# Where the low parts of the first expert's first weights are made, in a two-layer mixture-of-experts kernel

## Chip, cores and metric

The program runs on one core of a Trainium2 chip. The metric is the device time of one execution in microseconds (us); lower is better.

## What is computed

An attention with 32 memory slots gives x, 4608 tokens of width 512. Two mixture-of-experts layers follow. In the first, every one of 8 experts gets exactly 576 tokens, by a greedy assignment in the order of the logits; in the second, every token goes to its best expert, with a gate. Cut to the first layer:

```python
logits = x @ w_gate
order = np.argsort(-logits.flatten())
for idx in order:
    tok, e = idx // E, idx % E
    if assigned[tok] >= 0 or counts[e] >= cap:
        continue
    assigned[tok] = e
    counts[e] += 1
for e in range(E):
    h = np.maximum(x[assigned == e] @ w1[e], 0.0)
    out[assigned == e] = h @ w2[e]
```

## The kernel before

Products of the expert layers need more than one float32r product: a weight piece of 512 KB (128 x 1024) is loaded as `wraw`, ScalarE writes its rounded part (`w0h` or `w1h`, "0" for w1 of the reference and "1" for w2), and another engine writes the rest, `w0l` or `w1l` = raw minus rounded part. `Weights.split` (line 1282) does both. Four pieces make one expert's matrix.

The program has three stretches. (1) Attention, to about 120 us. (2) The routing of the first layer, about 120 to 168 us: four rounds of `Route1.guess` on VectorE. In a round, `propose` makes each token's proposal (lines 400 to 404, operations over 128 x 288), `counts` (line 410) sums it over the tiles, TensorE sums over the lanes (line 390, tile `rt`), and seven small operations (lines 427 to 435) make the new cutoffs. Beside the rounds, `beside` (line 1694) has TensorE compute what rows of x are still missing (line 259, tile `tr`), ScalarE copy them out (line 261, `xr`), SP store them to `xd`, SP load the first expert's four `w0` pieces, and, through `split`, ScalarE make `w0h` and GpSimd make `w0l`. TensorE, ScalarE and SP have their order as written there (`QUEUES`); in a round the rows stand ahead of the sums over the lanes in TensorE's queue, 3 rows ahead of the first sum and 1 or none ahead of the second.

Then `expert0` (lines 693 to 709) and `tables` make the tokens of the first two slots of 288: `slot0` gives the indices of slot 0, on which GpSimd's three gathers of `rows` hang (line 1326), `slot1` those of slot 1 (line 766), and, inside it, `check` counts the proposers once more (line 410 on VectorE, line 390 on TensorE, lines 499 and 500) and sets a flag. All engines read the flag and branch on it (`rest`, lines 524 and 525); with the given data it is 0 and the further rounds are left out. `first_x` then turns the gathered rows into slot 0's x: three copies on VectorE (line 1336), transposes on TensorE (line 1340), rounded part on ScalarE (line 1342), rest on VectorE (line 1343); x lies where the `w1` parts will lie later and so is called w1h and w1l there. After it, ScalarE's queue loads the four `w1` pieces into the same four places of `wraw`.

(3) The slots, from 168 us to the end: `mm1` (lines 1371 to 1374) has eight steps f of 12 products, steps 2k and 2k+1 with piece k of w0; ScalarE (line 1376, `hh`) and VectorE (line 1377, `hl`) empty its four PSUM banks; `mm2` follows (lines 1385 to 1387). In slot 0 VectorE also makes tables for the other slots (lines 656 to 661, 777, 789), which TensorE multiplies (line 783) between the steps, in nine products to a group.

Of the kernel before, what the change touches and what calls it, by code (L numbers as in the profile page):

```python
# [14 lines left out]
B, H, S, D, M = 8, 8, 576, 64, 32       # batches, heads, tokens of a batch, head width, memory slots  # L15
P = 128
N = B * S                               # tokens
NT = N // P
DM = H * D
E, F = 8, 1024                          # experts, their width  # L20
# [6 lines left out]
# pieces of the rows of x that a step computes, at three places  # L27
# [3 lines left out]
def chunks(b):  # L31
    """Token tiles of a batch: (tile, first lane, last lane, first s)."""
    if b % 2 == 0:
        t = b * S // P
        return [(t + i, 0, P, i * P) for i in range(4)] + [(t + 4, 0, 64, 512)]
    t = (b * S - 64) // P
    return [(t, 64, P, 0)] + [(t + 1 + i, 0, P, 64 + i * P) for i in range(4)]


def attention(tc, kv, qT, phiT, wg_sb, ident, xd, lg, keep, work, psum):  # L40
    """Logits of all tokens into lg. Returns what computes the rows of x of a batch, from
    the attention weights and value sums that stay in `keep`."""
# [31 lines left out]
    def ahead(s):  # L74
        """What step s is to use, in that order."""
        for f, b in ((load_q, s), (load_kv, s + 1), (load_phi, s + 2)):
            if 0 <= b < B:
                f(b)
# [21 lines left out]
    def a2(b):  # L100
# [3 lines left out]
        for j0 in range(0, 5, 2):  # L104
            js = list(range(j0, min(5, j0 + 2)))
            pt = psum.tile([P, 512], FT, name="tr", bufs=3).rearrange("p (a g c) -> p a g c", a=2, g=2)
            for j in js:
                t, l0, l1, s0 = cs[j]
                n = l1 - l0
                for g in range(2):  # L110
                    if n == P:
                        nc.tensor.transpose(pt[:, j - j0, g], e[:, g, s0:s0 + P], ident)
                    else:
                        # the lanes keep their place: out rows l0..l1
# [40 lines left out]
    def a4b(b):  # L155
# [3 lines left out]
        # keys: head u of a pair on partitions 64u.., columns 32u..  # L159
# [33 lines left out]
    def half(i, k, mid, end):  # L193
        """VectorE's part of a half's softmax: the first part of i beside the second part of k."""
# [5 lines left out]
        if k is not None:  # L200
# [5 lines left out]
            # column = token's place in the tiles of 128  # L206
# [139 lines left out]
def bc_e(a):  # L346
    """[128, 8] over the token tiles."""
    return a[:, None, :].to_broadcast([P, NT, E])


def bc_t(a):
    """[128, 36] over the experts."""
    return a[:, :, None].to_broadcast([P, NT, E])


class Route1:
    """Every expert takes its 576 best of the tokens that its betters left.

    A token proposes to the best expert whose cutoff it reaches. An expert never takes a
    token below the 576th of those that propose to it, so its cutoff can be raised to any  # L360
    value that 576 of its proposers reach; once no expert has more than 576 proposers, they
    are the greedy assignment."""

    def __init__(self, tc, pool, psum, lg, cn):
# [11 lines left out]
        # -1 on the lane itself and those before  # L376
# [9 lines left out]
    def total(self, src, n):  # L386
        """Sums over the lanes, on every lane."""
# [24 lines left out]
    def guess(self, first, beside):  # L412
        """A new cutoff, the proposers' mean, where there are too many of them."""
# [23 lines left out]
    def step(self):  # L437
        """The same, but only where 576 or more reach the pivot; between the cutoff and `hi`
        the pivots halve what is left."""
# [26 lines left out]
        # a new cutoff where 576 or more of too many proposers reach the pivot  # L466
# [10 lines left out]
        # below the pivot, or from the top again where 576 have come to lie above  # L477
# [11 lines left out]
    def check(self):  # L489
        """flag = 1 unless every expert has 576 proposers, which then are the assignment:  # L490
        each token is with one expert, and all that it would rather be with are full of
        better ones, however the cutoffs came about."""
# [4 lines left out]
        ps = self.total(part[:, 0:8], 8)  # L497
        d = self.tmp("d", [1, 24])
# [3 lines left out]
    def resolve(self, beside, per=4):  # L502
        """Some rounds; what they come to is the assignment if the flag, which check() sets, is 0."""
# [4 lines left out]
    def rest(self, after, blocks=8, per=4):  # L508
        """Where the flag is set: rounds until it isn't, at last one expert after the other; then after()."""
# [21 lines left out]
    def general(self):  # L531
        """One expert is filled at a time, at the highest logit at which one gets full;
        of equal logits there the first tokens are taken."""
# [18 lines left out]
        def first_of(x, w):  # L552
            # of the entries that are 1, the first expert's
            v.tensor_tensor(x, x, w, op=OP.mult)

        with tc.For_i(0, E + 1):
# [43 lines left out]
            # everything above the level, and as many at it as the expert still takes  # L600
# [19 lines left out]
    def ranks(self, src):  # L620
        """How many entries of the same expert come before, in the order of the tokens."""
# [3 lines left out]
def lane_sums(r1, src):  # L625
    """Of src [128, tile, expert]: sums over the lanes, and less those of the lane itself and the later ones."""
# [8 lines left out]
def prefix(r1, sums, per_expert):  # L635
    """Of a src of 0 and 1: the count of ones in earlier tiles or lower lanes,
    per expert, or with the experts before it (per_expert False); [128, tile, expert]."""
# [13 lines left out]
def split_pos(nc, tmp, pos, cn, oh):  # L651
    """pos div 32, and in oh the one-hot of pos mod 32."""
# [12 lines left out]
def pause(n):  # L665
    """Steps without work, for an engine to get done what the next one reads."""
    for _ in range(n):
        yield


class Invert1:
    """From the assignment to the tokens of the positions: idx [(q, t'), block of 32 positions]
    = 4 token + q, and in tok the token's lane and tile for the partition (s mod 4, t'),
    column (s div 4, block in slot)."""
# [11 lines left out]
    def expert0(self, beside=lambda: None):  # L686
        """The first expert's tokens alone, which are those of the first two slots."""
# [9 lines left out]
        # the place, from 1024 on; 0 where the token is another expert's  # L697
# [13 lines left out]
    def places(self):  # L711
        """The place of every token."""
# [8 lines left out]
    def slot(self, s):  # L721
        """[mod 32, (lane, 128 tile), block] of the tokens of a slot's positions."""
# [18 lines left out]
    def slot0(self, beside=lambda: None):  # L741
        """The first slot's tokens: position 128 c + lane at (lane, c)."""
# [14 lines left out]
    def slot1(self, beside=lambda: None):  # L757
        """The second slot's part of idx."""
# [9 lines left out]
    def all(self, r2):  # L768
# [33 lines left out]
        # the lane and the tile of the token, for each quarter of the partitions  # L802
# [12 lines left out]
def constants(tc, pool, ident=None):  # L815
# [27 lines left out]
    # rep[k, a, 32 q + t] = 1 where k = 32 a + t  # L843
    rep = t("rep", [64, 2, P], FT)
    rt = t("rept", [64, P], FT)
    for a in range(2):
        # (column mod 32) + 32 a - k
# [7 lines left out]
NS = 23                     # slots of 288 that 8 experts can need for 4608 tokens  # L855
NE = 27                     # columns of tokens, of 36, that are through six experts
AS = 5                      # slots that they fill for certain
G = 9
# [7 lines left out]
class Route2:  # L866
    """Every token to its best expert; the experts' tokens fill slots of 288.

    Tokens lie in the first layer's order: lane (s mod 4, t), column (s div 4, block).
    A token's place is its rank with its expert, moved by whole slots."""  # L870
# [30 lines left out]
    def choose(self, j0, j1):  # L901
        """The first of the best experts for the columns j0..j1."""
# [19 lines left out]
    def gates(self, j0, j1):  # L922
        """Softmax of the choice times sigmoid of its output gate, in three bfloat16 parts."""
# [29 lines left out]
    def ranks(self, j0, j1, before):  # L953
        """Of the tokens of the columns j0..j1: rank with their expert, as (div 32, mod 32)."""
# [47 lines left out]
    def left(self, j0):  # L1002
        """One-hot (place mod 32) times what the place is to know, for G columns."""
# [18 lines left out]
    def per_token(self, c, a, out):  # L1022
        """a [128, 8] of the tokens' experts."""
# [8 lines left out]
    def slots(self, k, tab, w):  # L1032
        """The slots before each expert's, from how many it has; the slots' experts.

        k may go twice over the experts."""
# [731 lines left out]
```

## Time and profile before

| what | us |
|---|---|
| median of the runs | 1065.51 |
| all three runs | 1065.51, 1063.35, 1068.17 |
| span of the profiled execution, first to last instruction | 1063.4 |
| attention and what comes before the routing | 0 to about 120 |
| routing of the first layer, to slot 0's first product | about 120 to 168 |
| slots of both layers | 168 to 1063.4 |

The profiled execution is listed with its span alone; the span is within 0.1 us of the lowest of the three runs and 2.1 us below their median, so that hardly any time lies around it. Over the span TensorE is busy 990.5 us (93%), VectorE 663.7 (62%), ScalarE 486.4 (46%) and GpSimd 565.6 (53%). In the table of windows and in timelines, PE is TensorE's products, PEld its weight loads, DVE VectorE, ACT ScalarE, POOL GpSimd; an arrow with an engine names what ended the idle time before an instruction. PEclk is the granted clock of TensorE, 1.00 for 2.4 GHz and 0.50 for 1.2 GHz.

### The profile page before, as it was taken

To read this page: it belongs to the slowest core of one execution; us is meant where nothing else is said; L and a number is where in the kernel's file an instruction comes from. 1 tells how busy PE (TensorE), PEld (TensorE's weight loads), DVE (VectorE), ACT (ScalarE), POOL (GpSimd) and SP (SyncE) were. 2 spreads that over 40 slices of the span, in tenths; PEclk is the share of its full clock that TensorE was granted. 3 is DMA by queue.
4 is the path that set the end of the run, shared out by engine and by line. 5 is a ranking of instruction groups with operands and counts; after the bars stand their busy time and mean duration, and the time that the engine had idled before them with its cause. 6 is when DMAs were issued, how large, how long until landed. Compare 5 with 4: busy or idle time off the path is not lost. (4 is left out here: it accounts for less than half of the span.)

```text
span 1063.4 us, 21285 instructions
## 1 busy us (share of the span) xinstructions
PE 990.5 (93%) x8163; PEld 936.4 (88%) x8163; DVE 663.7 (62%) x1181; ACT 486.4 (46%) x906; POOL 565.6 (53%) x545
## 2 busy tenths in 40 slices
PE   6778968999999999999999999999999898989974
PEld 4555648999999999999999999999999898989962
DVE  3888875554545454547964798666665665656641
ACT  3546623343434333333333557555555554546530
POOL 3102033243434343434443487778887787878875
PEclk9889967999999999999999999999999999989987
DMA  8999744344343435352525656566666565656663
GB/s 311 367 339 298 237 142 139 120 129 141 108 140 109 147 102 151 102 162 85 152 95 160 189 193 207 185 203 216 201 204 219 183 201 181 204 180 201 201 211 115
DMA packets 77544, 192.16 MB, mean 181 GB/s; under 512 B 13884, under 2 KB 32320, under 8 KB 76400
## 3 DMA queue, kind: packets, MB, share of 16 engines
q1 hardware_dynamic: 62448, 158.93, 46.1%
q0 software_dynamic: 14400, 29.59, 8.5%
q10 hardware_dynamic: 576, 2.10, 0.5%
q8 instruction: 69, 1.13, 0.4%
q14 instruction: 51, 0.42, 0.1%
HBM read 162.25 MB, written 28.44 MB: 179 GB/s over the span
## 5 line engine op out<-in xcount | busy, mean ns | idle before, releaser
L1385 PE MATMUL py<-hh,w1h 128*128 128x288 f32 x1024 | 304.7, 298 | 12.4 <-DVE yr L1397 12.4
L1386 PE MATMUL py<-hl,w1h 128*128 128x288 f32 x1024 | 305.6, 298 | 0.1
L1387 PE MATMUL py<-hh,w1l 128*128 128x288 f32 x1024 | 305.0, 298 | 0.0
L1371 PE MATMUL ph<-xh,w0h 128*128 128x288 f32 x992 | 273.0, 296 | 0.0
L1372 PE MATMUL ph<-xh,w0l 128*128 128x288 f32 x992 | 271.5, 296 | 0.0
L1318 POOL DMA_INDIRECT xg<-xd,idx x135 | 147.8, 1095 | 217.9 <-DVE xt L1349 151.1
L1376 ACT ACTIVATE hh<-ph 128x288 fp32r<-128x288 f32 x256 | 104.9, 411 | 232.3 <-PE ph L1374 232.1
L1385 PEld LDWEIGHTS py<-hh,w1h 128*128 128x128 f32 x1024 | 195.7, 191 | 13.9 <-DVE yr L1397 13.6
L1386 PEld LDWEIGHTS py<-hl,w1h 128*128 128x128 f32 x1024 | 195.5, 191 | 0.5 <-DVE hl L1377 0.5
L1377 DVE SCALAR_TENSOR_TENSOR hl<-ph,hh 128x288 fp32r<-128x288 f32 x256 | 116.1, 454 | 127.5 <-ACT hh L1376 127.3
L1387 PEld LDWEIGHTS py<-hh,w1l 128*128 128x128 f32 x1024 | 195.6, 191 | 0.0
L1371 PEld LDWEIGHTS ph<-xh,w0h 128*128 128x128 f32 x992 | 186.4, 188 | 2.4 <-issue 2.1
L1372 PEld LDWEIGHTS ph<-xh,w0l 128*128 128x128 f32 x992 | 186.4, 188 | 0.2 <-issue 0.2
L1374 PE MATMUL ph<-xl,w0h 128*128 128x288 f32 x992 | 171.3, 294 | 0.0
L1318 POOL DMA_INDIRECT xg<-x2d,r2gidxB x118 | 145.8, 1235 | 36.4 <-issue 32.3
L1286 DVE TENSOR_TENSOR w0l<-wraw,w0h 128x1024 fp32r<-128x1024 f32 x96 | 117.0, 1218 | 48.8 <-ACT w0h L1285 48.7
L1374 PEld LDWEIGHTS ph<-xl,w0h 128*128 128x128 f32 x992 | 145.2, 188 | 0.0
L1286 DVE TENSOR_TENSOR w1l<-wraw,w1h 128x1024 fp32r<-128x1024 f32 x100 | 120.6, 1206 | 24.8 <-ACT w1h L1285 24.7
L1485 POOL DMA_INDIRECT out_dram<-yr,r2sidxB x99 | 117.8, 1189 | 32.0 <-issue 18.9
L1285 ACT ACTIVATE w1h<-wraw 128x1024 fp32r<-128x1024 f32 x100 | 105.4, 1054 | 46.3 <-PE py L1386 25.1
L1285 ACT ACTIVATE w0h<-wraw 128x1024 fp32r<-128x1024 f32 x100 | 103.4, 1050 | 0.4 <-DMA wraw<-in_u_dram 0.4
L1394 ACT ACTIVATE yT<-py 128x288 f32<-128x288 f32 x64 | 26.4, 412 | 128.5 <-PE py L1387 128.5
(319 smaller groups left out, 1056.6 us busy)
## 6 DMA issues: line engine op xcount, KB each, us to landing
wraw<-in_u_dram SPq DMA_DIRECT2D x140, 512.0 KB, 4.2
wraw<-in_w_dram SPq DMA_DIRECT2D x60, 512.0 KB, 3.7
kvt<-in_kv_dram SPq DMA_DIRECT2D x16, 1024.0 KB, 15.8
q<-in_qT_dram SPq DMA_DIRECT2D x8, 1152.0 KB, 18.4
x2d<-yr SPq DMA_DIRECT2D x64, 144.0 KB, 2.4
xd<-xr SPq DMA_DIRECT2D x32, 256.0 KB, 2.6
ph<-in_phiT_dram SPq DMA_DIRECT2D x8, 576.0 KB, 18.3
xg<-xd,idx POOLq DMA_INDIRECT x135
```

Source lines behind the costliest of these rows:

```text
L1285: self.nc.scalar.activation(h, r, AF.Copy)
L1286: (eng or self.nc.vector).tensor_tensor(l, r, h.bitcast(FT), op=OP.subtract)
L1318: self.nc.gpsimd.indirect_dma_start(out=x[:, j], out_offset=None, in_=src, in_offset=bass.IndirectOffsetOnAxis(ap=idx[:, j:j + 1], axis=0))
L1371: nc.tensor.matmul(ps, wh[:, o + c], xh[:, c], start=(c == 0), stop=False)
L1372: nc.tensor.matmul(ps, wl[:, o + c], xh[:, c], start=False, stop=False)
L1374: nc.tensor.matmul(ps, wh[:, o + c], xl[:, c], start=False, stop=(c == 3))
L1376: nc.scalar.activation(hh[:, f], ps, AF.Relu)
L1377: nc.vector.scalar_tensor_tensor(hl[:, f], ps, 0.0, hh[:, f].bitcast(FT), op0=OP.max, op1=OP.subtract)
L1385: nc.tensor.matmul(ps, wh[:, f], hh[:, f], start=(f == 0), stop=False)
L1386: nc.tensor.matmul(ps, wh[:, f], hl[:, f], start=False, stop=False)
L1387: nc.tensor.matmul(ps, wl[:, f], hh[:, f], start=False, stop=(f == 7))
L1485: i = nc.gpsimd.indirect_dma_start(out=os, out_offset=bass.IndirectOffsetOnAxis(ap=idx[:, j:j + 1], axis=0), in_=y[:, j], in_offset=None, ...
```

## The change

`split` takes which parts it is to make, and the low part is always VectorE's. In the rounds only the rounded parts are made. Piece 0's low part is put into `check`, between the product that sums the count over the lanes and the operation that reads this sum. The low parts of pieces 1 to 3 come behind `first_x`, ahead of the loads of the `w1` pieces.

```diff
-    def split(self, which, k, eng=None):
+    def split(self, which, k, parts="hl"):
         r = self.raw()[:, k].rearrange("p a b -> p (a b)")
         h, l = (a[:, k].rearrange("p a b -> p (a b)") for a in self.all(which))
-        self.nc.scalar.activation(h, r, AF.Copy)
-        (eng or self.nc.vector).tensor_tensor(l, r, h.bitcast(FT), op=OP.subtract)
+        if "h" in parts:
+            self.nc.scalar.activation(h, r, AF.Copy)
+        if "l" in parts:
+            self.nc.vector.tensor_tensor(l, r, h.bitcast(FT), op=OP.subtract)
...
-    def check(self):
+    def check(self, beside=lambda: None):
...
         ps = self.total(part[:, 0:8], 8)
+        beside()
         d = self.tmp("d", [1, 24])
...
                     if 0 < k < 5 and i == 0:
-                        w.split(0, k - 1, nc.gpsimd)
+                        w.split(0, k - 1, "h")
...
-                def tables():
+                def tables(beside=lambda: None):
                     inv.slot0(inv.places)
-                    inv.slot1(r1.check)
+                    inv.slot1(lambda: r1.check(beside))
...
+                def low(ks):
+                    for k in ks:
+                        w.split(0, k, "l")
...
                 with tc.manual_schedule(engines=ALL):
-                    tables()
+                    tables(lambda: low((0,)))
                 r1.rest(again)
                 with tc.manual_schedule(engines=ALL):
                     sl.first_x(rows0, cols0, psum, cn["ident"])
+                    low((1, 2, 3))
                     for k in range(4):
                         w.load(1, k, 0, queue=nc.scalar)
```

Line numbers of the changed kernel are up to 3 higher here: 1289 is its line of the low part, 1281 that of a load, 1339, 1346 and 1380 answer to 1336, 1343 and 1377, and 500, 501 and 767 to 499, 500 and 766.

GpSimd's queue from the routing's first constants to the read of the flag, before:

```order
L381 IOTA r1m_1579 128x648
L1286 TENSOR_TENSOR w0l_1657<-wraw_1589,w0h_1656 128x1024 x4
L1326 DMA rows_1834<-xd,idx_1781 128x512 x2
L1326 DMA rows_1834<-xd,idx_1781 32x512
L524 TENSOR_LOAD r1flag
```

and after:

```order
L380 IOTA r1m_1578 128x1152
L381 IOTA r1m_1579 128x648
L1329 DMA rows_1830<-xd,idx_1778 128x512 x2
L1329 DMA rows_1830<-xd,idx_1778 32x512
L525 TENSOR_LOAD r1flag
```

The four subtractions are gone from GpSimd; its next work is the gathers.

VectorE around the check (`r1td` reads the summed count), before:

```order
L730 TENSOR_TENSOR r1tR_1898<-r1tR_1898,c_tile_83 128x324
L410 TENSOR_REDUCE r1tpart<-r1prop 128x8
L499 TENSOR_SCALAR r1td<-rt 1x8
L500 TENSOR_REDUCE r1flag<-r1td 1x1
L766 TENSOR_SCALAR idx_1782<-rt,c_q 128x9
L524 TENSOR_LOAD r1flag
```

and after:

```order
L731 TENSOR_TENSOR r1tR_1894<-r1tR_1894,c_tile_83 128x324
L410 TENSOR_REDUCE r1tpart<-r1prop 128x8
L1289 TENSOR_TENSOR w0l_1657<-wraw_1589,w0h_1656 128x1024
L500 TENSOR_SCALAR r1td<-rt 1x8
L501 TENSOR_REDUCE r1flag<-r1td 1x1
L767 TENSOR_SCALAR idx_1779<-rt,c_q 128x9
L525 TENSOR_LOAD r1flag
```

One subtraction stands between the count over the tiles and the read of its sum over the lanes.

VectorE from slot 0's x into slot 0's products, before:

```order
L1336 COPY cols_1835<-rows_1834 32x512
L1343 TENSOR_TENSOR w1l_4090<-tr,w1h_4089 128x4x128 x2
L1343 TENSOR_TENSOR w1l_4090<-tr,w1h_4089 128x4x32
L1377 SCALAR_TENSOR_TENSOR hl_4172<-ph_4173,hh_4171 128x288
L656 TENSOR_SCALAR r2xhi<-pos 128x36
```

and after:

```order
L1339 COPY cols_1831<-rows_1830 32x512
L1346 TENSOR_TENSOR w1l_4087<-tr,w1h_4086 128x4x128 x2
L1346 TENSOR_TENSOR w1l_4087<-tr,w1h_4086 128x4x32
L1289 TENSOR_TENSOR w0l_1657<-wraw_1589,w0h_1656 128x1024 x3
L1380 SCALAR_TENSOR_TENSOR hl_4172<-ph_4173,hh_4171 128x288
L657 TENSOR_SCALAR r2xhi<-pos 128x36
```

Three subtractions stand ahead of the first `hl`.

ScalarE's queue at the same place, with the engines whose semaphores each instruction waits for, before:

```order
L1342 ACTIVATE w1h_4089<-tr 128x4x128 [waits PE_49] x2
L1342 ACTIVATE w1h_4089<-tr 128x4x32 [waits PE_49]
L1280 DMA wraw_1589<-in_w_dram 128x1024 [waits Pool_49] x4
L1376 ACTIVATE hh_4171<-ph_4173 128x288 [waits DVE_49,PE_49]
L1376 ACTIVATE hh_4171<-ph_4174 128x288 [waits PE_49]
```

and after:

```order
L1345 ACTIVATE w1h_4086<-tr 128x4x128 [waits PE_49] x2
L1345 ACTIVATE w1h_4086<-tr 128x4x32 [waits PE_49]
L1281 DMA wraw_1589<-in_w_dram 128x1024 [waits DVE_49] x3
L1281 DMA wraw_1589<-in_w_dram 128x1024 [waits DVE_49,Activation_49]
L1379 ACTIVATE hh_4171<-ph_4173 128x288 [waits PE_49]
```

The four loads of `w1`, which overwrite what the subtractions read, waited for GpSimd and now wait for VectorE, each for its piece, and the first `hh` is queued behind them.

## Rows read from the trace of the kernel before

**Rows 1.** The first line of the page.

```profile
span 1063.4 us, 21285 instructions
```

**Rows 2.** Windows: per engine busy us (instructions), then PEclk, DMA share, GB/s.

```profile
138.00:140.00 2.00, 2.00 (x6) 1.43 (x5) 1.86 (x5) 0.60 (x1) 0.00 (x0) 0.50 0.00 0
169.00:1064.00 895.00, 861.73 (x6740) 847.80 (x6739) 537.46 (x895) 407.79 (x724) 527.79 (x459) 0.98 0.51 164
```

**Rows 3.** Timeline of GpSimd in the routing: start, us, engine, line, what, idle before.

```profile
129.81 2.34 POOL L1286 TENSOR_TENSOR w0l<-wraw,w0h 128x1024 fp32r<-128x1024 f32 x1 [23.86 <-ACT w0h L1285]
133.19 2.46 POOL L1286 TENSOR_TENSOR w0l<-wraw,w0h 128x1024 fp32r<-128x1024 f32 x1 [1.04 <-ACT w0h L1285]
143.90 2.36 POOL L1286 TENSOR_TENSOR w0l<-wraw,w0h 128x1024 fp32r<-128x1024 f32 x1 [8.24 <-ACT w0h L1285]
147.83 2.63 POOL L1286 TENSOR_TENSOR w0l<-wraw,w0h 128x1024 fp32r<-128x1024 f32 x1 [1.57 <-ACT w0h L1285]
```

**Rows 4.** Timeline of VectorE in the routing.

```profile
125.25 0.46 DVE L401 SCALAR_TENSOR_TENSOR r1masked<-r1tlt,lg 128x288 f32<-128x288 f32 x1
129.95 2.52 DVE L401 SCALAR_TENSOR_TENSOR r1masked<-r1tlt,lg 128x288 f32<-128x288 f32 x1
134.07 1.90 DVE L422 TENSOR_TENSOR r1tpv<-r1masked,r1prop 128x288 f32<-128x288 f32 x1
142.35 0.17 DVE L427 TENSOR_SCALAR r1tu<-rt 128x8 f32<-128x8 f32 x1 [1.67 <-PE rt L390]
143.91 2.37 DVE L435 TENSOR_TENSOR r1cut<-r1cut,r1tu 128x8 f32<-128x8 f32 x1
148.89 0.19 DVE L700 TENSOR_TENSOR r1tx<-r1tx,lg 128x36 f32<-128x36 f32 x1
149.11 1.42 DVE L701 TENSOR_TENSOR r1tx0i<-r1tx,r1prop 128x36 int32<-128x36 f32 x1
```

**Rows 5.** Timeline of TensorE in the routing.

```profile
128.65 2.84 PE L259 MATMUL tr<-vbd,eT 128*128 128x256 f32 x12
136.75 5.45 PE L259 MATMUL tr<-vbd,eT 128*128 128x256 f32 x12
152.70 2.27 PE L733 MATMUL rt<-r1tR,r1toh 128*32 128x18 bf16 x36 [1.38 <-DVE r1tR L730]
```

**Rows 6.** Timeline of VectorE from the check into slot 0.

```profile
159.24 0.15 DVE L499 TENSOR_SCALAR r1td<-rt 1x8 f32<-1x8 f32 x1 [1.90 <-PE rt L390]
164.71 1.10 DVE L1336 COPY cols<-rows 128x512 f32<-128x512 f32 x3 [4.08 <-DVEq L525]
167.83 0.89 DVE L1343 TENSOR_TENSOR w1l<-tr,w1h 128x512 fp32r<-128x512 f32 x2 [0.16 <-ACT w1h L1342]
171.82 0.46 DVE L1377 SCALAR_TENSOR_TENSOR hl<-ph,hh 128x288 fp32r<-128x288 f32 x1 [3.10 <-ACT hh L1376]
180.83 0.59 DVE L789 TENSOR_SCALAR r2R<-c_i,r2sm 128x144 bf16<-128x144 bf16 x3
211.19 1.23 DVE L1286 TENSOR_TENSOR w0l<-wraw,w0h 128x1024 fp32r<-128x1024 f32 x1 [0.55 <-ACT w0h L1285]
```

**Rows 7.** Timeline of GpSimd: last gathers of `rows` and of slot 1, one beside VectorE's subtraction.

```profile
159.59 0.88 POOL L1326 DMA_INDIRECT rows<-xd,idx  x1 [0.30 <-issue]
175.18 1.37 POOL L1318 DMA_INDIRECT xg<-xd,idx  x1 [0.30 <-issue]
211.60 1.63 POOL L1318 DMA_INDIRECT xg<-xd,idx  x1 [0.30 <-issue]
```

**Rows 8.** Timelines in slot 0: ScalarE's loads and first `hh`; TensorE.

```profile
167.77 1.90 ACTq L1280 DMA_DIRECT2D wraw<-in_w_dram  x4
171.37 0.41 ACT L1376 ACTIVATE hh<-ph 128x288 fp32r<-128x288 f32 x1 [3.33 <-PE ph L1374]
...
173.37 0.29 PE L1371 MATMUL ph<-w1h,w0h 128*128 128x288 f32 x1
181.35 0.75 PE L783 MATMUL rt<-r2R,r2L 128*64 128x144 bf16 x9
```

## Prediction

> **What bounds the kernel now.** I read the windows by stage first, then the timelines of the engines in the routing. In the slots TensorE is busy 861.73 of 895 us [rows 2]: there it is the bound, and whatever lets the first slot begin earlier moves the end by as much, since all later work hangs on its products in a fixed order. So the question is what sets slot 0's start. In the routing that is one chain on VectorE: each round needs the cutoffs of the one before, the indices need the last proposals, the gathers need the indices, the branch needs the flag.
>
> In that chain the reader is to see four operations that last far longer than their like. Line 401 takes 0.46 us in one round and 2.52 in the next, line 422, over the same 128 x 288, 1.90, line 435 2.37 where an operation of its size takes 0.17, and line 701 1.42 where its neighbour takes 0.19 [rows 4]. Laid beside GpSimd's timeline, each overlaps one of the four subtractions and ends within 0.4 us of it: 129.95 to 132.47 beside 129.81 to 132.15, 134.07 to 135.97 beside 133.19 to 135.65, 143.91 to 146.28 beside 143.90 to 146.26, 149.11 to 150.53 beside 147.83 to 150.46 [rows 3, 4]. I read this as VectorE being held until GpSimd's operation is over.
>
> The Trainium skill, page "SBUF — State Buffer", section "Who interferes with whom", says that a VectorE instruction with two SBUF inputs and a GpSimd instruction that reads SBUF exclude each other, the later one waiting for the whole of the earlier. The trace agrees: the four held ones read two SBUF tiles, and line 700, with one input in PSUM, is not held at 0.19 us [rows 4].
>
> **What is removed.** Four GpSimd subtractions of 2.34 to 2.63 us [rows 3]. GpSimd's own time is worth nothing, it idles there. VectorE's chain loses the stretch: 2.52 - 0.46 = 2.06, 1.90 - 0.46 = 1.44, 2.37 - 0.17 = 2.20, 1.42 - 0.19 = 1.23, together 6.93 us.
>
> A wait goes with it. In the fourth round VectorE idles 1.67 us for the sum over the lanes (line 427, [rows 4]), because TensorE has three rows of x in front of that sum, and they take 5.45 us where the same 12 products took 2.84 before [rows 5]: the granted clock was 0.50 at 138 to 140 us [rows 2], after TensorE had stood almost idle from 131.5 (128.65 + 2.84) to 136.75, waiting for VectorE. With the first two stretches gone (3.50 us), the sum behind which these rows stand, and with it the rows, come at 136.75 - 3.50 = 133.25 [rows 5]; the idle time shrinks from 5.2 to 1.7 us, and I take it that the clock stays up. Then the rows end at 133.25 + 2.84 = 136.1, and VectorE, which wants the sum at 142.35 - 1.67 - 3.50 = 137.2, doesn't wait: 1.67 us more. What is late next is the third row behind that sum: TensorE's next three rows (2.84 us) then end just about when the last proposals are ready, and I take off 0.3 for it, an estimate from these starts. Gain of the rounds and the first indices: 6.93 + 1.67 - 0.3 = 8.3 us.
>
> **What is added at the check.** One subtraction, 1.23 us on VectorE [rows 6]. It begins when the idle time ahead of line 499 begins, 159.24 - 1.90 = 157.34, and would end at 158.6; the sum is there at 159.24. So it costs nothing, with 0.7 us to spare. If that cover were gone, the flag would be late by at most 1.23. It does meet GpSimd's gathers: one beside a subtraction takes 1.63 against 0.88 [rows 7], so the last gather of rows ends at 161.2 instead of 160.5 (159.59 + 0.88). VectorE touches those rows only after the branch, at 164.71 [rows 6], and is held there by the branch: nothing again. The loads and stores on SP and ScalarE's rounded parts keep their order; GpSimd's queue only gets shorter.
>
> The Trainium skill's page "SBUF — State Buffer", section "A bandwidth-pool intuition that's wrong (but worth ruling out)", speaks against such a place: it gives about 620 ns for a GpSimd-issued DMA alone and 3100 ns beside a VectorE copy. By that figure one gather would be late by about 2.5 us, an estimate, and the sum worse by some 0.5; the row with 1.63 us [rows 7] bears out a much smaller delay for this very pair.
>
> **What is added behind x.** Three subtractions of 1.23, from the end of line 1343 at 167.83 + 0.89 = 168.72 to about 172.4 [rows 6]. Four waits follow. (a) Products of step 2 begin at 173.37 [rows 8] and want piece 1's low part, ready by 169.9; pieces 2 and 3 are wanted two and four steps later: no cost. (b) The loads of w1 now wait for VectorE, and the fourth leaves at 172.4 instead of within 167.77 to 169.67 [rows 8]; its piece is wanted by products over 20 us later: no cost. (c) Behind these loads on ScalarE stands the first `hh`, at 172.9 (172.4 and a quarter of 1.90) instead of 171.37 [rows 8], and with it VectorE's first `hl` and all that follows there is 1.5 us late. The PSUM bank that they empty is wanted again four steps on, after 176: no cost. (d) The tables that VectorE makes between those steps are late by about as much; the last three of TensorE's first group of nine end at 180.83 + 0.59 = 181.42, and the nine products run from 181.35 to 182.1 [rows 6, 8]. The ninth starts at about 182.0, so it has 0.6 us to spare and would be 0.9 late. I take 0.7, with a little caught up on the way, between 0 (VectorE catches up in time) and 1.5 (the whole lateness).
>
> **Sum.** 8.3 - 0.7 = 7.6 us. The profiled span of 1063.4 [rows 1] becomes 1055.8; from the median of the runs, 2.1 higher, 1065.5 - 7.6 = 1057.9.
>
> **Rivals.** *The clock stays up for longer.* With TensorE fed more densely up to the indices, the two groups of 36 small products that lead to the indices (2.27 us each, [rows 5]) could run at the upper level. Bounds: nothing, if their length isn't the clock's, to half of each, 2.3 us in all; with VectorE's chain in slot 0 capping what is won behind it, and 0.7 not lost, 10.6 us at most: 1054.9. Against it: TensorE waits for VectorE there in any case. 10%.
>
> *The clock falls all the same.* The rows show it at the lower level after 5.2 us almost idle; whether 1.7 us do it they don't show. Then the three rows take 5.45 again, the sum comes at 133.25 + 5.45 = 138.7, and of the 5.2 us by then won only 3.5 stay; the row behind the sum costs about 0.8 more (half of its share of 5.45 / 3). 8.3 - 1.7 - 0.8 - 0.7 = 5.1: 1060.4. 14%.
>
> *The stretch isn't GpSimd's doing*, and the operations stay long: no gain, 0.7 lost, 1066.2. Against it stand four of four coincidences in rows 3 and 4. 4%.
>
> *GpSimd holds VectorE in the other direction*: slower. Behind the branch GpSimd issues slot 1's nine gathers in a row, the last from 175.18 to 176.55 [rows 7]. If the three subtractions had to wait for that burst as operations waited for GpSimd in the rounds, piece 1's low part would come at 177.8 instead of 169.9, ScalarE would be stuck behind the loads until 180.7, and the tables, 9.6 us after the first `hl` (171.82 to 181.42), would hold TensorE for about 9.3. From 8.3 us of such waiting on the change loses: 1065.5 - 8.3 + 9.3 = 1066.5, and with the clock at half in some 4 us behind the idle time 1068.5, with the second rival on top 1071. Against it: the subtraction beside a gather took 1.23, and the gather gave way, 1.63 [rows 6, 7]. 6%.
>
> **How the numbers follow.** My forecast, 6 to 9.5 us won, has 66%. A change of 0.5%, 5.3 us, is about what a measurement of this kernel can tell. Faster by more than that: 65% from the forecast, 10% from the first rival, 5% from the second's better part, 80%. Within it: the rest of the second, the third, a little of the others, 15%. Slower: 5%. The likeliest time is 1057.9. The range goes down to 1053.5, the first rival's 1054.9 with the scatter of the runs, and up to 1062.5, the second rival's 1060.4 with 2 us of scatter (the three runs lie within 4.8); it leaves out the third and fourth.
>
> **What would show it.** In the changed kernel's routing: no operation of lines 400 to 435 over 0.75 us (the four held ones at 0.46, 0.46, 0.17, 0.19); no wait ahead of line 427 in the fourth round and PEclk at 1.00 in the rows there; the wait ahead of line 500 shorter by the subtraction but not gone; slot 0's first product near 160 instead of 168; the first `hh` waiting for the loads, not for TensorE; the last of nine products of line 783 waiting for VectorE. I am wrong if the rounds keep their length, if TensorE waits at step 2, or if a gather or a store of x, not VectorE's chain, sets when the copies of x begin.

## The result and the profile after

The changed kernel takes 1055.36 us, the median of five runs from 1053.64 to 1060.85. Five runs of the kernel before on the same chip have their median at 1065.51. The ratio is 0.9915, with a 95% interval from 0.9892 to 0.9938. The sign came as predicted, and the time lies 2.5 us below the 1057.9 us forecast, inside the range from 1053.5 to 1062.5.

**The span** is 9.9 us shorter than in [rows 1]. The execution whose span this is took 1055.36 us, so 1.9 us lie around the span; the text ahead of the prediction took it that hardly any do, since the span before happens to equal the lowest of the runs. First line of the page of the changed kernel:

```profile
span 1053.5 us, 21276 instructions
```

**VectorE's timeline** of the changed kernel, with start, duration, line and what is computed. The first six rows answer to [rows 4], the rest to [rows 6]:

```profile
129.28 0.46 DVE L401 SCALAR_TENSOR_TENSOR r1masked<-r1tlt,lg 128x288 f32<-128x288 f32 x1
131.33 0.45 DVE L422 TENSOR_TENSOR r1tpv<-r1masked,r1prop 128x288 f32<-128x288 f32 x1
136.41 0.16 DVE L427 TENSOR_SCALAR r1tu<-rt 128x8 f32<-128x8 f32 x1
138.01 0.17 DVE L435 TENSOR_TENSOR r1cut<-r1cut,r1tu 128x8 f32<-128x8 f32 x1
140.53 0.23 DVE L700 TENSOR_TENSOR_SCAN r1tx<-c_one,lg 128x36 f32<-128x36 f32 x1 [0.39 <-PE lg L695]
141.02 0.22 DVE L702 TENSOR_TENSOR r1tx0i<-r1tx,r1prop 128x36 int32<-128x36 f32 x1
...
147.89 1.21 DVE L1289 TENSOR_TENSOR w0l<-wraw,w0h 128x1024 fp32r<-128x1024 f32 x1
149.88 0.15 DVE L500 TENSOR_SCALAR r1td<-rt 1x8 f32<-1x8 f32 x1 [0.77 <-PE rt L390]
...
155.11 1.16 DVE L1339 COPY cols<-rows 128x512 f32<-128x512 f32 x3 [3.85 <-DVEq L526]
...
159.07 3.49 DVE L1289 TENSOR_TENSOR w0l<-wraw,w0h 128x1024 fp32r<-128x1024 f32 x3
163.47 0.46 DVE L1380 SCALAR_TENSOR_TENSOR hl<-ph,hh 128x288 fp32r<-128x288 f32 x1 [0.92 <-ACT hh L1379]
```

The four long operations of [rows 4] have the length of their like: 2.52, 1.90, 2.37 and 1.42 us have become 0.46, 0.45, 0.17 and 0.22. Line 427 waits for nothing. The subtraction at 147.89 ends at 149.10, and line 500 still waits 0.77 us for TensorE's sum behind it.

**TensorE's timeline**, against [rows 5], and in slot 0 against [rows 8]:

```profile
132.56 2.98 PE L259 MATMUL tr<-vbd,eT 128*128 128x256 f32 x12
...
143.41 2.27 PE L734 MATMUL rt<-r1tR,r1toh 128*32 128x18 bf16 x36 [1.03 <-DVE r1tR L731]
...
158.53 0.61 PE L1374 MATMUL ph<-w1h,w0h 128*128 128x288 f32 x1 [0.37 <-ACT w1h L1345]
...
172.21 1.00 PE L784 MATMUL rt<-r2R,r2L 128*64 128x144 bf16 x9
```

The three rows of x that took 5.45 us take 2.98. Slot 0's first product stands at 158.53; before, it stood at 168.09:

```profile
168.09 0.61 PE L1371 MATMUL ph<-w1h,w0h 128*128 128x288 f32 x1 [0.37 <-ACT w1h L1342]
```

**Windows** of the changed kernel (per engine busy us and instructions, then PEclk, DMA share, GB/s), against [rows 2]:

```profile
138.00:140.00 2.00, 2.00 (x11) 1.65 (x10) 1.85 (x5) 1.23 (x3) 0.00 (x0) 1.00 0.43 108
144.00:146.00 2.00, 1.74 (x33) 1.64 (x33) 1.61 (x4) 0.18 (x1) 0.00 (x0) 1.00 0.31 116
148.00:150.00 2.00, 1.86 (x31) 1.74 (x29) 1.23 (x2) 0.18 (x1) 1.62 (x2) 0.50 0.32 74
169.00:1053.00 884.00, 853.78 (x6683) 840.29 (x6681) 532.39 (x886) 404.05 (x718) 521.52 (x453) 0.98 0.53 163
```

The clock stays at its upper level through the rounds and falls at 146 to 148 us. In the slots TensorE is busy 853.78 of 884 us, the same 96 to 97% as before.

**ScalarE's queue and GpSimd** behind the check, against [rows 8] and [rows 7]:

```profile
158.20 4.78 ACTq L1281 DMA_DIRECT2D wraw<-in_w_dram  x4
163.03 0.41 ACT L1379 ACTIVATE hh<-ph 128x288 fp32r<-128x288 f32 x1 [4.55 <-DVE w0l L1289]
...
147.47 1.19 POOL L1329 DMA_INDIRECT rows<-xd,idx  x1 [41.88 <-DVE r1tR L731]
148.97 0.96 POOL L1329 DMA_INDIRECT rows<-xd,idx  x1 [0.30 <-issue]
...
161.41 1.97 POOL L1321 DMA_INDIRECT xg<-xd,idx  x1 [0.31 <-issue]
```

**Where the time went.** The table counts from the routing's first operation (line 403), which began at 120.46 us before and at 119.78 after. The starts are those of the timelines. `yr` is the turned result of a slot's `mm2`, so that slot 0's first `yr` comes behind all eight steps of its `mm1`. VectorE's timeline at both places, before and after:

```profile
120.46 0.45 DVE L403 TENSOR_REDUCE r1ttop<-lg 128x36 f32<-128x288 f32 x1
187.54 0.48 DVE L1397 STREAM_TRANSPOSE yr<-yT 128x288 f32<-128x288 f32 x1 [0.50 <-ACT yT L1394]
...
119.78 0.45 DVE L403 TENSOR_REDUCE r1ttop<-lg 128x36 f32<-128x288 f32 x1
178.65 0.48 DVE L1400 STREAM_TRANSPOSE yr<-yT 128x288 f32<-128x288 f32 x1 [0.49 <-ACT yT L1397]
```

| start of | before, us | after, us | earlier by |
|---|---|---|---|
| third round (line 400) | 9.00 | 9.01 | 0 |
| fourth round | 17.23 | 13.72 | 3.51 |
| last proposals | 25.85 | 18.44 | 7.41 |
| scan for the first indices (before 699, after 700) | 28.16 | 20.75 | 7.41 |
| first use behind the last long operation (703, 704) | 30.11 | 21.50 | 8.61 |
| read of the count (499, 500) | 38.78 | 30.10 | 8.68 |
| copies of x behind the branch (1336, 1339) | 44.25 | 35.33 | 8.92 |
| slot 0's first product (1371, 1374) | 47.63 | 38.75 | 8.88 |
| slot 0's first `yr` (1397, 1400) | 67.08 | 58.87 | 8.21 |

So 8.6 us are won in the rounds, 0.2 at the branch, and 0.7 are given back in slot 0. With the 0.68 us by which the routing began earlier, which lies ahead of the change, slot 0's first `yr` is 8.89 us earlier in the span. That lead, taken at each slot's first `yr`, is between 8.85 and 8.94 us in every slot up to slot 27 and 9.37 in slot 31. At the end it is 9.9.

### The profile page after: what moved, and what is told of

Read it like the earlier page. It is cut to its first block, busy times and chain, and to the rows that moved or that the text cites. A ratio compares the mean times of both kernels' runs of the same rounds, so it can differ in the third digit from the quotient of the medians.

```text
span 1053.5 us, 21276 instructions
## 1 busy us (share of the span) xinstructions
PE 987.7 (94%) x8163; PEld 935.7 (89%) x8163; DVE 661.4 (63%) x1185; ACT 486.2 (46%) x906; POOL 556.6 (53%) x541
## 5 line engine op out<-in xcount | busy, mean ns | idle before, releaser
L1289 DVE TENSOR_TENSOR w0l<-wraw,w0h 128x1024 fp32r<-128x1024 f32 x100 | 121.7, 1219 | 48.1 <-ACT w0h L1287 47.9
```

The costliest lines, as they stand in the source:

```text
L1289: self.nc.vector.tensor_tensor(l, r, h.bitcast(FT), op=OP.subtract)
```

## The experiments

They ran on three other chips, where the kernel before takes 1099.73 us (the first four below), 1115.53 (the next four) and 1100.23 (the last). So each time is compared with that of the kernel before on the same chip. The routing is compared by the traces: counted from line 403, the kernel before reached the third and fourth round and the last proposals at 9.01, 17.25 and 25.78 us on the chip of 1115.53 us, as in the table within 0.1. Behind the routing chips agree less well: slot 0's first product came at 48.21 us there, against 47.63. Where no other kernel is named, places in the traces are compared with the kernel before on the first chip.

**The halves.** The theory is a sum of separate stretches: whoever moves two subtractions wins those two. Low parts 2 and 3 alone on VectorE, where the third argument of `split` is the engine of the low part, or True for the high part alone and False for the low part alone:

```
-                        w.split(0, k - 1, nc.gpsimd)
+                        w.split(0, k - 1, nc.gpsimd if k < 3 else True)
...
                     sl.first_x(rows0, cols0, psum, cn["ident"])
+                    for k in (2, 3):
+                        w.split(0, k, False)
```

> Pieces 0 and 1 stay on GpSimd in the rounds, pieces 2 and 3 are VectorE's behind slot 0's x. Theory (GpSimd's subtraction holds VectorE, and the idle time that this gives TensorE lowers its clock): the operations of lines 401 and 422 stay at about 2.5 and 1.9 us, the three rows of x behind them stay slow (5.45 us) and the wait ahead of line 427 stays at 1.7; lines 435 and 701 fall to 0.2. Slot 0's first product comes 3.4 us earlier than before, counted from the first operation of the routing; total about 1062. Rival 1 (the time goes to something else than GpSimd's subtraction, such as the loads beside it): 435 and 701 stay long, no gain. Rival 2 (all gain hangs on the clock): nothing is gained, since the clock still falls.

Timelines of VectorE and of TensorE in that kernel:

```profile
129.83 2.49 DVE L401 SCALAR_TENSOR_TENSOR r1masked<-r1tlt,lg 128x288 f32<-128x288 f32 x1
133.91 1.94 DVE L422 TENSOR_TENSOR r1tpv<-r1masked,r1prop 128x288 f32<-128x288 f32 x1
141.26 0.17 DVE L427 TENSOR_SCALAR r1tu<-rt 128x8 f32<-128x8 f32 x1 [0.71 <-PE rt L390]
...
136.63 4.49 PE L259 MATMUL tr<-vbd,eT 128*128 128x256 f32 x12
```

The first two long operations are there as before, and the other two are gone. The wait at line 427 is 0.71 us where I had expected the old 1.67: TensorE's clock fell here too, but it rose again between 139.5 and 139.75 us, while the three rows still ran (last row of the fence, TensorE), so that they took 4.49 us and not 5.45. The two stretches that went, 2.20 + 1.23, and 0.96 of the wait make 4.4; line 703 came 4.3 us earlier, and slot 0's first product 3.6, of an expected 3.4. The time was 1096.09 against 1099.73, ratio 0.9948 (0.9912 to 0.9984). The other half, with part 0 in the check, part 1 behind x, and parts 2 and 3 left on GpSimd:

```
+                        w.split(0, k - 1, nc.gpsimd if k > 2 else True)
...
+                    tables(lambda: w.split(0, 0, False))
...
+                    w.split(0, 1, False)
```

> The other half: pieces 0 and 1 are VectorE's, in the check and behind slot 0's x; 2 and 3 stay on GpSimd in the rounds. Theory: lines 401 and 422 at 0.46, the three rows of x of the fourth round at 2.8 to 3.0 us, granted clock 1.00 there, no wait ahead of line 427: 5.2 us won up to line 427. Then the two subtractions left hold whichever operations with two SBUF inputs they meet, by 1.2 to 2.3 us each, so that the first product comes about 5 us earlier and the total is about 1060.5. The two halves add up to the whole, 8.6. Rival (the gain is the clock's alone): 1.7 us won, not 5.2.

Timeline of GpSimd and of VectorE:

```profile
137.68 2.35 POOL L1289 TENSOR_TENSOR w0l<-wraw,w0h 128x1024 fp32r<-128x1024 f32 x1 [32.17 <-ACT w0h L1287]
...
138.03 2.02 DVE L434 TENSOR_TENSOR r1tu<-r1tpivot,r1tu 128x8 f32<-128x8 f32 x1
...
143.09 1.43 DVE L702 TENSOR_TENSOR r1tx0i<-r1tx,r1prop 128x36 int32<-128x36 f32 x1
```

The two subtractions that stayed now meet lines 434 and 702, and hold these until they end: 138.03 + 2.02 = 140.05, beside 137.68 + 2.35 = 140.03. Line 427 does not wait. The routing up to line 704 is 5.5 us shorter and slot 0's first product 5.4 us earlier. The time, 1100.69 against 1099.73 with a ratio of 1.0006 (0.9964 to 1.0047), does not show this gain. The profiled run of this kernel took 1091.77, while others took up to 1106.89, so I take the total as inconclusive and the trace for the step. The halves win 4.3 + 5.5 = 9.8 where the whole wins 8.6. Of the 1.2 too much, 0.96 is the part of the one wait at line 427 that both take away, and 0.35 comes from the third hold, which is 1.85 us at line 434 where it was 2.20 at line 435.

**The wait by itself.** All subtractions stay on GpSimd, and 24 products whose result nobody reads are put, twelve at each of two places, where TensorE stood idle in the third round:

```
+                def keep_up(n):
+                    pk = psum.tile([P, 512], FT, name="pk", bufs=1)
+                    for _ in range(n):
+                        nc.tensor.matmul(pk[:, 0:288], cn["ones"], r1.m32[:, 0:8].rearrange("p a b -> p (a b)"),
+                                         start=True, stop=True)
...
+                    if k == 2:
+                        keep_up(12)
```

> The kernel before, with GpSimd's subtractions in place, and 24 products of 288 columns that nobody reads, in TensorE's idle time of the third round, 12 ahead of each sum over the lanes. Theory: the four long operations stay long; TensorE's clock stays at 1.00 into the fourth round, its three rows of x take about 2.9 us instead of 5.45, the wait of 1.67 us ahead of line 427 goes, and the first product comes 1.7 us earlier, counted from the routing's first operation. Rival (the three rows are slow because they wait for ScalarE or a transfer): they stay at 5.4 and nothing is won.

Timelines of TensorE and VectorE, then a window (columns as above):

```profile
132.28 1.63 PE L1696 MATMUL pk<-r1m,c_ones 128*128 128x288 bf16 x12
138.12 2.98 PE L259 MATMUL tr<-vbd,eT 128*128 128x256 f32 x12
...
130.14 2.32 DVE L434 TENSOR_TENSOR r1tu<-r1tpivot,r1tu 128x8 f32<-128x8 f32 x1
```

```profile
138.00:140.00 2.00, 1.91 (x9) 1.44 (x8) 1.72 (x9) 0.60 (x1) 0.00 (x0) 1.00 0.18 72
```

The clock stays up, the rows take 2.98 us as in the changed kernel, and line 427 does not wait. The four holds remain: lines 434, 422, 434 and 701 at 2.32, 2.10, 1.74 and 1.72 us, which is 6.9 over their like. Line 703 comes at 28.43 us after line 403, 1.68 earlier than before, where the prediction's term is 1.67. So the wait was the clock's doing, and the clock fell because VectorE was held. Of the 1.7 us, 1.3 are left at slot 0's first product: from line 703 to the read of the count this kernel takes 9.1 us, where the kernel before took 8.7. The one run of 1105.02 us is no measure of a gain of that size.

**What in the subtraction holds VectorE.** In two kernels GpSimd did something else with the same tile at the same places: only writing it, or reading one tile. Where GpSimd subtracted, the line becomes:

```
+            self.nc.scalar.activation(l[:, 0:8], r[:, 0:8], AF.Copy)
+            eng.memset(l.bitcast(FT), 0.0)
```

> The kernel before, but GpSimd fills each low part with zeros instead of subtracting (it writes 128 x 1024 and reads nothing); ScalarE writes eight columns of it first, so that GpSimd's operation stands at the same places. This leaves the low parts of the first expert's first weights out. Theory (VectorE is held by a GpSimd operation that reads SBUF, as the Trainium skill's page "SBUF — State Buffer" has it): lines 401, 422, 435 and 701 are at 0.46, 0.46, 0.17 and 0.2 us and the first product comes 8.6 us earlier than before, as in the changed kernel; since VectorE has no subtractions to make, TensorE doesn't wait at line 783 and the first yr of slot 0 is earlier by 0.5 to 0.7 us more than in the changed kernel. Rival (any GpSimd operation holds VectorE): operations long by as much as GpSimd's operations last.

Timelines of GpSimd and of VectorE:

```profile
128.91 0.95 POOL L1290 MEMSET w0l<- 128x1024 f32 x1 [23.02 <-ACT w0l L1289]
...
129.30 0.46 DVE L401 SCALAR_TENSOR_TENSOR r1masked<-r1tlt,lg 128x288 f32<-128x288 f32 x1
```

Line 401 reads two SBUF tiles and lies whole inside the memset (128.91 to 129.86), and it has its 0.46 us. The rounds begin at 9.0, 13.71 and 18.42, as in the changed kernel. Slot 0's first product came 8.7 us earlier than before, of an expected 8.6. The profile's spans on GpSimd are rough, but the starts of the rounds don't hang on them. So it is not GpSimd's being busy, nor its writing, that holds VectorE. I had also looked for slot 0 to come out ahead of the changed kernel's here, and that did not show: the first `yr` stood at 60.0 after line 403, against 58.87. Its step with line 783 took 3.81 us (2.34 before on the first chip), and TensorE waited 1.08 us there for VectorE's tables, with no subtraction behind x. The kernel before has 4.03 there on the chip of 1115.53 us, while two kernels below have 2.40 on such chips. What disturbs the place stays open. The next kernel reads one input:

```
+            eng.tensor_copy(l, h.bitcast(FT))
```

> The kernel before, but GpSimd copies the rounded part into the low part's place (one SBUF input instead of two), so that the first expert's first weights have their rounded part twice and no low part. Theory (reading is what holds VectorE): operations with two SBUF inputs are held until GpSimd's copy ends, each by up to the copy's length; if the copy is as long as the subtraction, 2.4 us, nothing is won against before. Rival (two GpSimd inputs are needed): no operation is held.

```profile
130.39 1.04 POOL L1289 CAST w0l<-w0h 128x1024 fp32r<-128x1024 f32 x1 [23.20 <-ACT w0h L1285]
...
130.57 1.17 DVE L401 SCALAR_TENSOR_TENSOR r1masked<-r1tlt,lg 128x288 f32<-128x288 f32 x1
...
143.86 1.04 POOL L1289 CAST w0l<-w0h 128x1024 fp32r<-128x1024 f32 x1 [3.57 <-ACT w0h L1285]
...
143.91 1.03 DVE L707 CAST r1tsm<-r1tx0h 128x36 bf16<-128x36 int32 x1
```

Line 401 is held by 0.71 us until 0.3 after the copy's end, and the rounds begin at 9.01, 14.45 and 19.47 us after line 403 instead of 9.0, 13.71 and 18.42. What reads SBUF on GpSimd holds VectorE, and for as long as it lasts, so a copy of 1.04 us costs less than a subtraction of 2.35. The single runs of the two kernels, 1088.0 and 1114.98 us, are no measure of such differences. The Trainium skill's page "SBUF — State Buffer", section "Who interferes with whom", says that a two-input VectorE instruction contends with GpSimd's reads of SBUF but not with its writes; both rows agree. The last row of the fence was unexpected and is told of below.

**The kernel before and the changed kernel again**, both unaltered, on the chip of 1115.53 us:

> The kernel before, for its profile on the chip of the three others: the four long operations of lines 401, 422, 435 and 701 and the wait of 1.7 us ahead of line 427 as in the first profile, whatever the span.

> The changed kernel unaltered, beside the next one on the same chip. About 0.85% below the kernel before; first product 8.9 us earlier than before counted from the routing's first operation, some 0.7 of it given back by the end of slot 0's first steps.

The four long operations of the kernel before last 2.49, 1.95, 2.36 and 1.42 us there, and its wait at line 427 is 1.58. The changed kernel took 1106.34 against 1115.53, ratio 0.9904 (0.9874 to 0.9934). Its rounds begin at 9.0, 13.71 and 18.43, its first product stands at 39.25 and its first `yr` at 59.36 us after line 403, where the kernel before has 48.21 and 69.21. So the gain is 9.0 us up to the first product, as on the first chip (8.9). In slot 0 the comparison is disturbed by a stall of the kernel before:

```profile
175.90 0.46 DVE L1377 SCALAR_TENSOR_TENSOR hl<-ph,hh 128x288 fp32r<-128x288 f32 x1 [2.27 <-issue]
```

VectorE waited 2.27 us there for nothing that the profile shows. What slot 0 gives back is therefore read from the first chip alone.

**The cover of the check, and the loss in slot 0.** If a second subtraction is put into the check's wait, it should run past the sum, by 1.2 less the 0.77 us to spare, and ScalarE's loads and first `hh` come free earlier. The last argument of `first_x` is called right behind the copies of x:

```
-                    tables(lambda: low((0,)))
+                    tables(lambda: low((0, 1)))
...
-                    sl.first_x(rows0, cols0, psum, cn["ident"])
-                    low((1, 2, 3))
+                    sl.first_x(rows0, cols0, psum, cn["ident"], lambda: low((2,)))
+                    low((3,))
```

> The changed kernel with the low parts spread: pieces 0 and 1 in the check's wait, piece 2 between the copies of slot 0's x and VectorE's part of its split (VectorE waits 1.14 us there), piece 3 behind. Theory (the 0.7 us given back in slot 0 come from VectorE's lateness and from ScalarE being held behind the loads): the flag is 0.4 us later, but line 767 and the branch are not; the first product is at most 0.1 us later; ScalarE's first hh waits for TensorE again and line 784's nine products take 0.75 us; the first yr comes 0.5 to 0.7 us earlier than in the changed kernel, total about 0.06% below it. Rival (what is given back comes from TensorE's clock or from the weights' transfers): the same 0.7 us are given back. Second rival (the check's wait doesn't hide two): the branch is 0.4 us later and eats what is won.

Timelines of TensorE, of VectorE and of ScalarE:

```profile
149.60 0.19 PE L390 MATMUL rt<-r1tpart,c_ones 128*128 128x8 bf16 x1
...
147.84 2.35 DVE L1289 TENSOR_TENSOR w0l<-wraw,w0h 128x1024 fp32r<-128x1024 f32 x2
151.01 0.15 DVE L500 TENSOR_SCALAR r1td<-rt 1x8 f32<-1x8 f32 x1 [0.82 <-PE rt L390]
155.88 1.17 DVE L1339 COPY cols<-rows 128x512 f32<-128x512 f32 x3 [3.90 <-DVEq L526]
...
158.94 2.51 ACTq L1281 DMA_DIRECT2D wraw<-in_w_dram  x4
162.54 0.41 ACT L1380 ACTIVATE hh<-ph 128x288 fp32r<-128x288 f32 x1 [3.34 <-PE ph L1378]
```

The cover holds one subtraction and not two: TensorE's sum ends at 149.79 and the two subtractions at 150.19, 0.4 us behind it. Line 500 begins another 0.82 us later. The profile puts that down to the sum, which was there by then, so it was something else: in the changed kernel on this chip line 500 begins 0.54 us behind the sum as well, on the first chip 0.04. Against the changed kernel on this chip line 500 is 0.7 us later, line 767 0.2, and the copies of x and the first product 0.37, where the theory had the branch in its old place. In return the loads are out in 2.51 us instead of 4.78, the first `hh` waits for TensorE again, and the nine products of line 784 take 0.75 us, as in [rows 8]; their step takes 2.40 us, against 3.20 in the changed kernel on this chip. The first `yr` came no earlier all the same, at 59.83 against 59.36: slot 0 began 0.37 later, and its second step took 2.73 us instead of 1.97, since the clock rose later. The time was 1107.82, ratio 0.9914 (0.988 to 0.9948): no better than the change as it is. A last kernel kept one subtraction in the check, put one behind the copies and two behind x:

```
+                    sl.first_x(rows0, cols0, psum, cn["ident"], lambda: low((1,)))
+                    low((2, 3))
```

> The changed kernel with piece 1's low part between the copies of slot 0's x and VectorE's part of its split, piece 0 in the check as in the changed kernel, pieces 2 and 3 behind. Theory (the check's wait hides one subtraction and not two, the wait behind the copies hides one, and what stands behind x holds ScalarE): the branch is where it is in the changed kernel, the first product at most 0.1 us later, ScalarE's loads end 1.1 us earlier and line 784's nine products are not torn apart by more than 0.3 us; 0.2 to 0.8 us by slot 0's first yr, which the total can't tell from the changed kernel (same as it, about 0.85% below the kernel before). Rival (the wait behind the copies is no cover): the first product is 1.1 us later.

Timelines of ScalarE and of VectorE:

```profile
158.33 3.64 ACTq L1281 DMA_DIRECT2D wraw<-in_w_dram  x4
162.01 0.41 ACT L1380 ACTIVATE hh<-ph 128x288 fp32r<-128x288 f32 x1 [3.42 <-PE ph L1378]
...
155.27 1.16 DVE L1339 COPY cols<-rows 128x512 f32<-128x512 f32 x3 [4.03 <-DVEq L526]
156.36 1.20 DVE L1289 TENSOR_TENSOR w0l<-wraw,w0h 128x1024 fp32r<-128x1024 f32 x1
```

The first `hh` waits for TensorE, and line 784 takes its 0.75 us, at no cost to the check. The first product comes 0.23 us later than in the changed kernel on the first chip, with a branch of 4.03 us instead of 3.85, and not 1.1 later, so the wait behind the copies is a cover. The step with line 784 takes 2.40 us instead of 2.65. But the second step took 2.76 instead of 2.38, and the first `yr` stood at 59.19, against 58.87. The time was 1088.83 against 1100.23, ratio 0.9911 (0.9877 to 0.9945). So ScalarE's delay can be had back, and it is worth no more than the scatter of slot 0's first steps.

## Why the prediction was right

**The four stretches** (6.93 us) were right in size and in cause. They are 2.06, 1.45, 2.20 and 1.20 by the two traces. That GpSimd's reading is the cause, and no coincidence, is shown by the halves and by the memset and the copy. The third rival, that the stretch is not GpSimd's, falls with them. Which operation is held, and for how long, hangs on where the subtraction meets VectorE: in the second of the halves and in the kernel with the added products it is line 434, for 2.02, 2.32 and 1.74 us, each time until the subtraction ends.

**The wait of 1.67 us** was right too. The prediction took it that TensorE's clock stays up when its idle time shrinks; the rows took 2.98 us at a granted clock of 1.00, and the kernel with the added products won 1.68 up to line 703 by the clock alone. The rows began at 132.56 us behind 1.9 us without rows, where 1.7 were forecast. The second rival is out.

**The third row behind the sum**, for which 0.3 us were taken off, cost nothing: line 700 follows the last proposals, which end at 140.15, after its usual wait of 0.39 us for TensorE. The rounds and first indices won 8.6 where 8.3 were forecast.

**The check** went as worked out: 0.77 us left of a forecast 0.7, and of two subtractions put there the second ended 0.4 us behind the sum. The gathers paid nothing: the two that overlap the subtraction take 1.19 and 0.96 us, where the prediction took 1.63, and before, with no subtraction beside them, the same two took 1.19 and 0.95. The Trainium skill's page "SBUF — State Buffer", section "A bandwidth-pool intuition that's wrong (but worth ruling out)", gives about 3.1 us for a GpSimd-issued DMA beside a VectorE copy. No gather took that here beside a subtraction, which is not a copy; the longest, beside the last of the three that begin at 159.07, took 1.97. The fourth rival needed VectorE to be held by the gathers: its three subtractions took 3.49 us in all, so it is out.

**Behind x** the sum was right by luck, and its parts were not. Forecast were 0.7 us, all at the ninth product of line 783; measured were 0.67 for slot 0. The mechanism is there: the first `hh` waits for the loads, which wait for `w0l`, and stands 4.50 us behind the first product instead of 3.28, 1.2 later of a forecast 1.5. The nine products take 1.00 instead of 0.75, the last three of them behind the tables that VectorE makes at 172.35 to 172.93, and their step 2.65 instead of 2.34: 0.31 us, so this term was taken more than twice too large. Another 0.14 is the second step, in which the clock rose 4.8 us behind the first product instead of 4.5. The rest, 0.22, is nearly all in four steps of 1.63 instead of 1.57 to 1.59. These vary as much without the change: the kernel before has 1.63 on the chip of 1115.53 us. So 0.3 of the 0.7 is the change's by the trace of the first chip; the rest isn't shown to be.

**The first rival**, that the small products shorten with the clock, had its condition met for the first of its two groups, and not its consequence. These 36 products of line 734 ran at a granted clock of 1.00 at 144 to 146 us, and took 2.27 us. Before they took the same 2.27, at 0.50, as this window of the kernel before shows:

```profile
152.00:154.00 2.00, 1.30 (x23) 1.32 (x24) 1.83 (x6) 0.00 (x0) 0.00 (x0) 0.50 0.35 131
```

**What the sum misses.** It said 7.6 us, and 6 to 9.5 as the forecast's own part of the chances; 9.9 were measured in the span and 10.15 between the medians. That is nearer to the first rival's 10.6, whose mechanism did not act. By the interval of the ratio the change is worth between 6.6 and 11.5 us, so the 7.6 isn't contradicted. Up to slot 0's first `yr` the change is worth 8.21: 0.3 more from the third row, and 0.23 from a branch that lasted 3.85 instead of 4.08 us, which scatters (3.90 and 4.03 in the last two kernels). The 0.68 us ahead of the routing isn't the change's: line 403 began anywhere between 119.4 and 121.5 us in the traces. The last microsecond, which comes in the branches of slots 28 to 31 and at the end, I could not lay to the change. It stays open whether it is scatter. So some 8.2 of the 9.9 us are accounted for.

## What to carry to other kernels

When an operation lasts several times as long as its like, lay the other engines' timelines beside it before looking at the operation itself: here an idle engine's cheap work was paid for on the engine that sets the end. Such work goes where the engine that it disturbs waits anyway, and the wait's length says how many pieces fit: one here, since two ended 0.4 us behind what was waited for. Count what the hold does one step on as well: the idle time that it made on TensorE lowered the clock, and that wait was a fifth of the gain.

## What the runs showed besides

- A VectorE cast of 128 x 36 with one input was held as well beside GpSimd's copy, 1.03 us instead of 0.17 (last row of the copy's kernel). I had expected that of operations with two inputs alone. The Trainium skill's page "SBUF — State Buffer", section "Who interferes with whom", names copies and casts among the operations that can take the port shared with GpSimd, where their operands meet certain conditions, and this row agrees.
- On the same 128 x 1024 values GpSimd takes 0.95 us for a memset, 1.04 for a copy and 2.35 for a subtraction; VectorE subtracts in 1.21.
- The length of 36 products of 18 columns, 2.27 us, isn't the clock's; that of twelve of 256 columns is, 2.84 to 2.98 at 1.00 and 5.45 at 0.50.
- On the other three chips the kernel before takes 3 to 5% longer. Each of the nine traces from them, whatever the kernel, shows 90 to 120 waits of TensorE or VectorE between 120 and 1000 us that are over 0.3 us long and that the profile puts down to "issue"; the two traces of the first chip show none. Their cause stays open.
